# Transposing transfers begun by ScalarE's queue in place of SyncE's, in a fused windowed-attention and feed-forward kernel

## The chip, the cores and the metric

The kernel runs on one core of one Trainium2 chip. The metric is the device time of one execution in microseconds; lower is better. The profile shows the core's engines by these names: PE (TensorE matmuls) and PEld (its weight loads), DVE (VectorE), ACT (ScalarE), POOL (GpSimd) and SP (SyncE), which only begins transfers. `SPq` and `ACTq` are the instruction queues of SP and ACT.

## The reference

```python
scores = scale * q @ k.T                       # (8 batches, 8 heads, 576, 576), head size 64
rel = pos[:, None] - pos[None, :]
mask_plain = (rel >= 0) & (rel < 32)                          # heads 0 to 3
mask_dil = (rel >= 0) & (rel < 128) & (rel % 4 == 0)          # heads 4 to 7
attn = softmax(where(mask, scores, -1e9))
x = (attn @ v) as (8, 576, 512)
xn = (x - mean) / sqrt(var + 1e-6) * g
out = x + relu(xn @ w1) @ w2                   # w1 512 x 2048, w2 2048 x 512
```

Everything is float32 on the outside. Each query sees 32 keys: the 32 last ones, or every fourth of the last 128.

## The kernel before, in words

The 8 x 576 rows are 36 tiles of 128 rows, nine to a batch. A tile goes through the attention (scores, softmax, values), then through the layer norm (`norm`), and is then transposed, so that its 512 features stand on the partitions. Three tiles make a block, and the feed-forward part (`ffn`) works on blocks: `up` multiplies the transposed block with w1 into `ps_f` (L597), ACT evicts it with a relu as a 16-bit `hh` (L603) and DVE as the remainder `hl` (L604), and `down` multiplies with w2 (L620) and adds x (L626). `ps_f` has four PSUM buffers.

Products are made in 16-bit halves: a float32 number is a high part and a remainder. So `norm` ends with two tiles, `xh`, a cast by ACT (L568), and `xl`, the remainder, made by POOL (L569). `transposes` (L572 to L576) then moves both through two transposing DMA transfers into `xT`, which has two buffers by turns of blocks. The second one lies in spare room of the tile `w1_sb`, and is called `w_sb` in the profile. That makes 72 such transfers, two for each tile.

Around that run other users of the same queues. SP begins all loads and stores: queries and keys (L175 and L186, into `qk` or `slot`), values (L194), the weights (L655), small copies of v between tiles (L247), the results (L634), and the `row` loads (L225). These belong to `scale_v`: it takes the values of up to nine tiles, squares and sums them on ACT (L226), sums over the tiles on DVE (L228) and over the partitions on PE (L230), which gives a scale for the 16-bit values of the batch (`sv`). The `row` tile has two buffers and is also the tile that `down` writes its result to. ACT also splits weights and values (L153), casts queries and keys (L308, L279) and computes the exponentials (L413, L451, L452).

What order all this is in is settled in two steps. The kernel gives each piece of work (`unit`) a due time by hand and writes the pieces out in that order. A scheduler at build time then orders the instructions of each engine, by a simulation of the engines; each engine runs its own list strictly in order, DMA starts included, and waits at the head of the list until the semaphores of that instruction are there. Eight semaphores serve all transfers by turns, whichever engine begins them, so that a transfer also waits for the one eight before it.

Of the kernel before, what the change touches and what calls it, by code (L numbers as in the profile page):

```python
# [17 lines left out]
P = 128  # L18
# [50 lines left out]
def attention_then_ffn(ctx: ExitStack, tc, qkv, masks, g, w1, w2, out):  # L69
    nc = tc.nc  # L70
# [501 lines left out]
    def transposes(t, blk, i):  # L572
        st = state[t]
        blk["xTh"], blk["xTl"] = xT[blk["b"] % 2][:, 0], xT[blk["b"] % 2][:, 1]
        for name, src in (("xTh", st["xh"]), ("xTl", st["xl"])):
            nc.sync.dma_start_transpose(out=blk[name][:, :, i * P : (i + 1) * P], in_=src)  # L576


    def ffn(blk, apart):
# [186 lines left out]
    for b in range(NBLK):  # L766
        blk = dict(t0=b * NB, b=b)
        for i in range(NB):
            t = b * NB + i
            if t < EARLY:  # L770
                t_at = TIMES["E"][t]
                if t:
                    unit(f"L{t}", t_at - 8.0, lambda t=t: load_tile(t), f"V{t - 2}")
                else:
                    unit("L0", 0.5, load_first)
                for n, (name, what) in enumerate((
                    ("S", scores_early), ("M", softmax_early), ("V", values_early), ("N", norm),
                )):
                    unit(f"{name}{t}", t_at + 3.0 * n, lambda t=t, what=what: what(t), f"L{t}", f"{name}{t - 1}")
                unit(  # L780
                    f"T{t}", t_at + 10.0, lambda t=t, i=i, blk=blk: transposes(t, blk, i), f"N{t}",
                    f"P{NFC // NW2 - 1}" if b else None,
                )
                if t == EARLY - 1:
                    unit(f"A{t}", TIMES["X"], lambda t=t: split_last(t), f"v{t}", f"N{t}")
                continue
# [12 lines left out]
            if t % TPP == 5 and t + 4 < NT:  # L799
# [4 lines left out]
            do("N", VALUES + 2, norm, f"V{t}")  # L804
            unit(
                f"T{t}", t_at + READY, lambda t=t, i=i, blk=blk: transposes(t, blk, i),
                f"N{t}", f"P{NFC // NW2 - 1}" if b else None, f"b{b - 2}",
            )
# [24 lines left out]
        else:  # L833
            when = max(start, units[f"T{b * NB + NB - 1}"][0] + 0.1, max(units[a][0] for a in last))
            for n, (took, what) in enumerate(ups + downs):
                name = f"b{b}" if n == len(ups) + len(downs) - 1 else f"b{b}.{n}"
# [76 lines left out]
```

## Time and profile before

| | |
|---|---|
| runs | 941.67 us, median of 3 (940.76 to 941.94) |
| profiled execution | 944.02 us, its span 942.2 us |
| PE busy | 890.7 us, 95% |
| DVE, ACT, POOL busy | 634.2, 312.7, 312.3 us |
| DMA engines | 42.3% of 16 engines' span, all on one queue |
| transposing transfers | 72, all begun by SP |

Times inside the span count from its start. Engines work side by side, so busy times don't add up; a group's row names the line, the engine, what is written and read, how often, and in the bracket how long the engine stood idle before it and what ended that. Beginning a transfer is not counted as busy time of an engine. Clock stands for the granted TensorE clock, 1.00 at full speed.

### The profile page before, as it was taken

The page shows a single profiled execution, that of the slowest core. Times are in us where ns is not written, and L with a number is a line of the kernel's source. Part 1 is how long each engine was busy: PE and PEld are TensorE (multiplying, and loading weights), DVE is VectorE, ACT ScalarE, POOL GpSimd, SP SyncE. Part 2 cuts the span into 40 slices and gives each one's busy share as a digit, 9 for nine tenths or more (in the row PEclk, how much of TensorE's full clock was granted, in tenths as well). Part 3 has the DMA queues.
Part 4 walks back from the last instruction along what each step waited for, and adds up shares of the span by engine and source line. Part 5 has one row for each costly group of instructions (what it writes and reads, how often), then busy time and mean ns, then how long its engine had stood idle before and what let it go on. Part 6 is the DMA issues. An engine that isn't in the chain of part 4 may idle for free.

```text
span 942.2 us, 18610 instructions
## 1 busy us (share of the span) xinstructions
PE 890.7 (95%) x7608; PEld 552.2 (59%) x7608; DVE 634.2 (67%) x1379; ACT 312.7 (33%) x588; POOL 312.3 (33%) x319
## 2 busy tenths in 40 slices
PE   4479789999999999999999999999999999999998
PEld 4379466777665555565565565565565565564553
DVE  4799658896977577786686686686686685660210
ACT  4556742334323343251241451241241341130110
POOL 1010273646234235454253353354243341120000
PEclk9979899999999999999999999999999999999999
DMA  7887872754344516446143654364043411010000
GB/s 241 311 229 229 187 176 50 153 122 115 66 75 93 148 52 133 92 71 136 37 80 71 169 105 71 89 123 90 30 88 69 87 27 37 21 24 23 12 1 34
DMA packets 79622, 93.39 MB, mean 99 GB/s; under 512 B 47920, under 2 KB 53680, under 8 KB 79536
## 3 DMA queue, kind: packets, MB, share of 16 engines
q1 hardware_dynamic: 79536, 92.21, 42.3%
q8 instruction: 59, 0.97, 0.4%
q14 instruction: 27, 0.22, 0.1%
HBM read 71.86 MB, written 9.44 MB: 86 GB/s over the span
## 4 chain that ended last, share of the span: by engine, by line
PE 81%; DMA 10%; ACT 3%; DVE 3%; issue 2%; SPq 1%; POOL 1%; ACTq 0%; DVEq 0%; POOLq 0%
PE ps_f L597 36%; PE ps_f L620 35%; PE ps_s L330 4%; PE ps_v L528 4%; DMA row<-in_qkv 4%; DMA slot<-in_w 3%; DMA xT<-xl 1%; ACT row L226 1%; DMA slot<-in_qkv 1%; DMA v<-in_qkv 0%; PE ps_f L673 0%; ACT w_sb L153 0%; DVE slot L662 0%; POOL slot L280 0%; DVE slot L154 0%
## 5 line engine op out<-in xcount | busy, mean ns | idle before, releaser
L620 PE MATMUL ps_f<-w_sb,hh 128*128 128x512 f16 x1152 | 345.0, 380 | 5.8 <-ACT w_sb L153 5.0
L597 PEld LDWEIGHTS <-w_sb 128*128 128x128 f16 x3072 | 256.0, 99 | 126.6 <-issue 4.6
L620 PE MATMUL ps_f<-w_sb,hl 128*128 128x512 f16 x576 | 219.1, 380 | 0.0
L597 PE MATMUL ps_f<-xT,w_sb 128*128 128x384 f16 (+1 forms) x1536 | 199.2, 289 | 2.9 <-DMA xT<-xh 2.4
L597 PE MATMUL ps_f<-w_sb 128*128 128x384 f16 (+1 forms) x1536 | 196.7, 287 | 0.0
L620 PEld LDWEIGHTS <-hh 128*128 128x128 f16 x1152 | 111.8, 98 | 131.5 <-issue 6.8
L603 ACT ACTIVATE hh<-ps_f 128x384 f16<-128x384 f32 (+1 forms) x184 | 91.1, 500 | 216.8 <-PE ps_f L597 216.8
L604 DVE SCALAR_TENSOR_TENSOR hl<-ps_f,hh 128x384 f16<-128x384 f32 (+1 forms) x184 | 100.2, 569 | 42.4 <-ACT hh L603 40.3
L620 PEld LDWEIGHTS <-hl 128*128 128x128 f16 x576 | 56.5, 98 | 67.1 <-issue 1.8
L362 DVE TENSOR_TENSOR sc<-ps_s,mask 32x256 f32<-32x256 f32 x128 | 53.6, 419 | 51.2 <-PE ps_s L330 49.8
L435 DVE STREAM_TRANSPOSE pt_d<-pk 32x256 f32<-32x256 f32 x128 | 79.4, 621 | 1.8
L626 DVE SCALAR_TENSOR_TENSOR row<-ps_f,s,x 128x512 f32<-128x512 f32 x36 | 27.0, 749 | 74.5 <-PE ps_f L620 74.0
L446 POOL TENSOR_TENSOR sc<-sc,mx 128x512 f32<-128x512 f32 x32 | 33.4, 1043 | 116.3 <-DVE mx L444 116.3
L451 ACT ACTIVATE p<-sc 128x512 f32<-128x512 f32 x32 | 20.2, 631 | 128.2 <-POOL sc L446 128.2
L569 POOL TENSOR_TENSOR xl<-xn,xh 128x512 f16<-128x512 f32 x36 | 42.0, 1166 | 59.1 <-ACT xh L568 49.8
L330 PE MATMUL ps_s<-slot 128*128 128x128 f16 (+1 forms) x768 | 58.8, 226 | 2.1 <-DVE sc L348 2.1
L330 PEld LDWEIGHTS <-slot 128*128 128x128 f16 x768 | 50.9, 99 | 12.7 <-DVE sc L348 3.0
L287 POOL COPY slot<-slot 128x128 f16<-128x128 f16 x56 | 17.5, 340 | 119.4 <-PE ps_v L528 119.3
L348 DVE TENSOR_TENSOR sc<-ps_s,mask 32x256 f32<-32x256 f32 x128 | 53.5, 418 | 4.9 <-PE ps_s L330 3.4
L453 POOL TENSOR_TENSOR pk<-p,pk 128x512 f16<-128x512 f32 x32 | 40.7, 1271 | 45.8 <-ACT pk L452 45.8
L458 DVE STREAM_TRANSPOSE pt_b<-pk 32x128 f16<-32x128 f16 x87 | 26.1, 300 | 42.0 <-ACT pk L452 28.4
L554 POOL TENSOR_TENSOR rstd<-rstd,mhalf 128x1 f32<-128x1 f32 x36 | 21.1, 587 | 94.9 <-DVE rstd L553 85.2
(100 smaller groups left out, 961.3 us busy)
## 6 DMA issues: line engine op xcount, KB each, us to landing
qk<-in_qkv SPq DMA_DIRECT2D x36, 512.0 KB, 6.9
slot<-in_qkv SPq DMA_DIRECT2D x32, 512.0 KB, 6.7
slot<-in_w SPq DMA_DIRECT2D x14, 1024.0 KB, 6.3
out_x<-row SPq DMA_DIRECT2D x36, 256.0 KB, 2.0
row<-in_qkv SPq DMA_DIRECT2D x33, 256.0 KB, 2.9
v<-in_qkv SPq DMA_DIRECT2D x33, 256.0 KB, 3.0
slot<-in_w SPq DMA_DIRECT2D x4, 512.0 KB, 7.3
slot<-in_qkv SPq DMA_DIRECT2D x28, 64.0 KB, 4.5
```

The source lines that it names most:

```text
L330: nc.tensor.matmul(out, lhs, rhs, start=(n == 0), stop=(n == len(terms) - 1))
L348: nc.vector.tensor_tensor(out=sc[pj, 0:HP, :], in0=ps[pj, :, W * j : W * j + 2 * W], in1=mask_16[pj, m : m + 1, :].broadcast_to([W, HP, 2 ...
L362: nc.vector.tensor_tensor(out=sc[pj, HP:H, :].rearrange("p h (t i) -> p h t i", t=2), in0=ps[pj].rearrange("p h (t c) -> p h t c", t=2)[:, ...
L435: nc.vector.transpose(dd[pj].rearrange("p t h (i r) -> p r t h i", r=DIL)[:, j], pk[pj, HP:H, :].rearrange("p h (t i) -> p t h i", t=2),)
L446: nc.gpsimd.tensor_tensor(out=sm, in0=sc, in1=mx.broadcast_to([P, H, 2 * W]), op=ALU.subtract)
L453: nc.gpsimd.tensor_tensor(out=pk16[:, :, :, 1], in0=p32, in1=pk16[:, :, :, 0], op=ALU.subtract)
L528: nc.tensor.matmul(oo, l, r, start=(n == 0), stop=(n == len(mm) - 1))
L569: nc.gpsimd.tensor_tensor(out=xl, in0=xn, in1=xh, op=ALU.subtract)
L597: nc.tensor.matmul(z[:, n], l, r, start=(m == 0), stop=(m == len(mm) - 1))
L603: nc.scalar.activation(hh, z, AF.Relu)
L604: nc.vector.scalar_tensor_tensor(out=hl, in0=z, scalar=0.0, in1=hh, op0=ALU.max, op1=ALU.subtract)
L620: nc.tensor.matmul(o, l, r, start=(f == 0 and m == 0), stop=(f == NFC - 1 and m == 2))
```

## The change

The two transposing transfers of a tile are begun by ACT's queue; SP no longer begins any of them. What is moved, where to and when it is needed stay the same.

```diff
@@ def transposes(t, blk, i):
         st = state[t]
         blk["xTh"], blk["xTl"] = xT[blk["b"] % 2][:, 0], xT[blk["b"] % 2][:, 1]
         for name, src in (("xTh", st["xh"]), ("xTl", st["xl"])):
-            nc.sync.dma_start_transpose(out=blk[name][:, :, i * P : (i + 1) * P], in_=src)
+            nc.scalar.dma_start_transpose(out=blk[name][:, :, i * P : (i + 1) * P], in_=src)
```

The scheduler orders all engines anew, so lists change in more than the 72 rows. On ACT, behind the exponentials of the fourth tile (t=3, 111 us in the profile), where the third tile is transposed:

```order
-L603 ACTIVATE hh<-ps_f 128x4x128
-L153 ACTIVATE w_sb<-w_sb,s_2_1539 128x2x512
+L576 DMA_TRANSPOSE xT<-xh 128x4x128
+L603 ACTIVATE hh<-ps_f 128x4x128
+L576 DMA_TRANSPOSE xT<-xl 128x4x128
 L308 CAST slot<-qk_1329 128x1024
 L279 CAST slot<-qk_1329 128x4x128
 L279 CAST slot<-qk_1329 128x512
-L226 ACTIVATE row,v_sums<-row 128x512 x2
-L153 ACTIVATE w_sb<-w_sb,s_2_1539 128x2x512
+L153 ACTIVATE w_sb<-w_sb,s_2_1539 128x2x512 x2
+L226 ACTIVATE row,v_sums<-row 128x512 x2
```

The two transfers stand around an eviction, and the two squares L226 have moved behind both splits of w2. A little further on the same list, the same happens to the last three squares of the batch:

```order
 L423 COPY pt_a_81<-ps_s 128x256
 L425 COPY pt_d_85<-ps_s 128x64 x4
-L226 ACTIVATE row,v_sums<-row 128x512 x2
 L153 ACTIVATE w_sb<-w_sb,s_3_1541 128x2x512
-L226 ACTIVATE row,v_sums<-row 128x512
+L226 ACTIVATE row,v_sums<-row 128x512 x3
```

They now follow the last split. On SP, at the same place (108 to 113 us):

```order
 L225 DMA row<-in_qkv 128x512 x2
-L576 DMA_TRANSPOSE xT<-xh 128x4x128
-L186 DMA slot<-in_qkv 64x2x1024
-L576 DMA_TRANSPOSE xT<-xl 128x4x128
-L186 DMA slot<-in_qkv 64x2x1024
+L186 DMA slot<-in_qkv 64x2x1024 x2
 L247 DMA v_b_84<-slot 32x4x64
 L194 DMA v_1662<-in_qkv 128x512
```

The two halves of a load of queries and keys now follow the row loads directly. On SP at the start of the third batch's row loads (310 us):

```order
 L186 DMA slot<-in_qkv 64x2x1024 x2
-L576 DMA_TRANSPOSE xT<-xh 128x4x128
-L225 DMA row<-in_qkv 128x512
-L576 DMA_TRANSPOSE xT<-xl 128x4x128
-L225 DMA row<-in_qkv 128x512
+L225 DMA row<-in_qkv 128x512 x2
 L634 DMA out_x<-row 128x512
 L225 DMA row<-in_qkv 128x512 x7
```

The first two row loads no longer stand behind and between the transfers of that tile.

## The prediction

> **What bounds the kernel now.** I read the page's busy line and slices first, then TensorE stage by stage, then its waits and the chain that ended last, and last the queues and engines that the moved transfers leave and join.
>
> ```profile
> span 942.2 us, 18610 instructions
> PE 890.7 (95%) x7608; PEld 552.2 (59%) x7608; DVE 634.2 (67%) x1379; ACT 312.7 (33%) x588; POOL 312.3 (33%) x319
> ...
> 100.00:125.00 25.00, 20.39 (x134) 10.21 (x134) 10.88 (x11) 21.19 (x46) 11.81 (x9) 0.86 0.93 210
> 125.00:150.00 25.00, 20.39 (x273) 17.94 (x272) 19.66 (x50) 7.73 (x14) 10.86 (x12) 0.93 0.66 121
> ...
> 310.00:337.00 27.00, 24.41 (x160) 14.49 (x159) 14.67 (x34) 11.29 (x29) 3.88 (x5) 1.00 0.61 157
> 337.00:341.00 4.00, 4.00 (x17) 1.97 (x15) 1.97 (x8) 2.00 (x4) 1.41 (x2) 0.57 0.00 2
> 341.00:900.00 559.00, 559.00 (x4101) 322.69 (x4100) 376.32 (x832) 161.53 (x294) 192.91 (x188) 1.00 0.34 72
> ```
>
> The columns of a stage are its bounds, its length, the busy time of PE, PEld, DVE, ACT and POOL, the granted clock, the DMA share and GB/s. From 341 to 900 us TensorE is busy 559.00 of 559.00 us: nothing that happens on SP or in the DMA engines there can shorten the time, it can only add. What can be won behind the loading phase lies mainly in two small places: 4.6 us idle in 125 to 150 (25.00 less 20.39), and 2.6 us in 310 to 337, after which the clock is 0.57 for 4 us, another 1.7 us (4 x 0.43). Stage 100 to 125 stands out the other way: ACT, the engine that takes over the transfers, is busy 21.19 of 25.00 us, and the DMA engines 0.93.
>
> ```profile
> PE ps_f L620 <- ACT w_sb L153: 5.0, 1, 5.0
> PE ps_v L230 <- DVE x L486: 4.6, 1, 4.6
> ...
> PE ps_f L597 <- DMA xT<-xh: 2.4, 2, 1.8
> ...
> PE ps_v L230 <- DVE v_tot L228: 2.1, 1, 2.1
> ```
>
> TensorE's own waits say the same (us in total, times, longest): the moved transfers (xT) keep it waiting for 2.4 us in all, while the two matmuls L230, which add up the squares of v, cost 4.6 us at 128 us and 2.1 us at 335 us. Both L230 end a chain of `row` loads, and both chains pass through SP just where it begins a transposing transfer.
>
> **The moved instructions.**
>
> ```profile
> L576 SPq DMA_TRANSPOSE xT<-xh x18: 1199/1231/1563, 50.0 to 776.8; - x18
> L576 SPq DMA_TRANSPOSE xT<-xl x18: 1194/1244/2067, 51.6 to 778.1; - x18
> ...
> DMA to landing us min/median/max: 2.4/5.8/9.1
> ```
>
> With the two groups into the second buffer there are 4 x 18 = 72, each 1.2 us of SP's time (median), so 72 x 1.24 = 89 us leave SP and join ACT, whose 312.7 us become some 402, 43% of the span (the page leaves issues out of its busy time). ACT's own price for beginning one does not stand in this trace; the bounds are 0.33 us, the shortest plain issue on SP (the row loads below), and 2.07 us, the longest transposing one. I take 1.24, the same instruction's. What counts is not the sum but what is queued behind each: the eviction L603 that frees TensorE's `ps_f`, the squares L226, the splits L153.
>
> **From 341 us on: 0.** Place after place looks like this.
>
> ```profile
> 474.63 0.62 ACT L568 CAST xh<-xn 128x512 f16<-128x512 f32 x1 [2.06 <-DVE xn L563]
> 475.15 0.48 ACT L603 ACTIVATE hh<-ps_f 128x384 f16<-128x384 f32 x1
> 476.87 0.49 ACT L603 ACTIVATE hh<-ps_f 128x384 f16<-128x384 f32 x1 [1.24 <-PE ps_f L597]
> 478.10 0.63 ACT L451 ACTIVATE p<-sc 128x512 f32<-128x512 f32 x1 [0.74 <-POOL sc L446]
> ...
> 475.32 1.16 POOL L569 TENSOR_TENSOR xl<-xn,xh 128x512 f16<-128x512 f32 x1 [1.31 <-ACT xh L568]
> ...
> ACT hh L603 <- PE ps_f L597: 216.8, 119, 32.5
> ```
>
> xh is ready at 475.25 and xl at 476.48, so the two issues need ACT until 477.7 at the latest, with an eviction between them or 0.9 us late. ACT has waited for TensorE 216.8 us in front of its evictions, and with four `ps_f` buffers, one filled in 1.7 us (the evictions at 475.15 and 476.87), TensorE can run on for some 4 us: three fillings less the eviction itself and DVE's share in it. A late eviction of 1 to 2.5 us is therefore hidden; if POOL were late with xl by 5 us it would not be, and that would cost 1 to 3 us a time. I take 0, with +3 as the upper end.
>
> **50 to 104 us: 0.** The first two pairs leave SP in this stretch. The xT waits above (at most 2.4 us) could shrink, or ACT's splits behind the pairs come up to 2.5 us later (two issues). Both end at the 5.0 us for which TensorE waits for ACT's first split of w2 behind this stretch; that split hangs on weight loads which the release of a `slot` sets free, not SP's turn.
>
> **108 to 133 us: +0.9.** This is where the change is decided, on the third tile's pair.
>
> ```profile
> 108.36 1.24 SPq L576 DMA_TRANSPOSE xT<-xh  x1
> ...
> 110.36 1.22 SPq L576 DMA_TRANSPOSE xT<-xl  x1
> 111.64 0.61 SPq L186 DMA_DIRECT2D slot<-in_qkv  x1
> ...
> 115.41 0.94 SPq L225 DMA_DIRECT2D row<-in_qkv  x2
> 120.63 1.28 SPq L186 DMA_DIRECT2D qk<-in_qkv  x2
> 123.44 0.33 SPq L225 DMA_DIRECT2D row<-in_qkv  x1
> ...
> row<-in_qkv SPq DMA_DIRECT2D x33, 256.0 KB, 2.9
> ...
> L153 ACT ACTIVATE w_sb<-w_sb,s 128x1024 f16<-128x1024 f32 x8 | 9.0, 1145 | 0.0
> ...
> 114.67 0.63 ACT L226 ACTIVATE row<-row 128x512 f32<-128x512 f32 x1
> ...
> 119.99 1.05 ACT L308 CAST slot<-slot 128x1024 f16<-128x1024 f32 x1 [1.91 <-DMA slot<-in_qkv]
> ...
> 122.66 0.67 ACT L226 ACTIVATE row<-row 128x512 f32<-128x512 f32 x1
> ...
> 130.35 0.63 ACT L226 ACTIVATE row<-row 128x512 f32<-128x512 f32 x1 [5.28 <-DMA row<-in_qkv]
> ```
>
> SP's side gains: without 1.24 + 1.22 us the second half of `slot` begins at about 109.2 in place of 111.64. ACT's side loses. In front of the two L226 of 114.67 there now stand two issues (2.46) and one split L153 more (1.15), so they come at about 118.2. Their `row` buffers are what the two loads of 115.41 wait for, so these come at about 118.9. L308 then starts at 119.4 to 119.99, about as before, since its load is there earlier. In front of the next squares there now stand two splits more (2.3), so these start at 124.4 to 125.0 in place of 122.66, and the last row load, begun at 123.44, comes 1.8 to 2.3 us later. It was 6.9 us under way (123.44 to 130.35), against a median of 2.9, because two 512 KB `qk` loads begun at 120.63 went ahead of it. If all of that excess is queueing it lands when it did, or 0.3 us sooner, the transposes being out of its queue; if none is, it lands 2.3 us later. Most of it is (4.0 of 6.9), so I take +0.9 out of -0.3 to +2.3. TensorE stands at L230 until then and has little idle time afterwards, so the delay goes through to the end.
>
> **310 to 337 us: 0.**
>
> ```profile
> 309.48 1.34 SPq L186 DMA_DIRECT2D slot<-in_qkv  x2
> 311.93 1.23 SPq L576 DMA_TRANSPOSE xT<-xh  x1
> 313.21 0.66 SPq L225 DMA_DIRECT2D row<-in_qkv  x1
> ...
> 312.00:314.00 2.00, 2.00 (x12) 0.98 (x11) 1.24 (x5) 0.00 (x0) 1.90 (x2) 1.00 1.00 240
> ...
> 313.21 5.23 DMA row<-in_qkv
> ...
> 336.42 0.17 DVE v_tot L228
> ```
>
> Here SP holds the first of nine row loads behind a transposing transfer that waits for xh until 311.93. Without it the load begins at about 310.9 (309.48 and 1.34), 2.3 us earlier, and five loads one after the other in the same buffer carry that to L230. But the DMA engines are full (1.00) while it waits, with 1 MB of `slot` ahead of it, and it lands behind that in any case: the 2.3 us go into a longer landing than 5.23, and the transposing bytes are merely shared differently. Bounds: -3.8 (all of the 2.1 us wait and 1.7 us of clock) and +0.7 (xl's bytes, which stood behind the row, now go beside it). I take 0.
>
> **Sum.** 0 + 0.9 + 0 + 0 = +0.9 us on the profiled execution: 944.02 (942.2 of span and 1.8 around it) becomes 944.9. It lies 2.35 us above the median of the runs, 941.67, so the forecast in runs is 942.6 us.
>
> The Trainium skill, "DMA: Bandwidth & Descriptors", section "Issuing engines are not separate DMA queues", speaks against the change: transfers begun by different engines run on the same 16 DMA engines, and a second issuer saves issue time only. By it alone the loads gain SP's 2.46 us at the third pair and no bandwidth, which is what the full DMA engines at 312 us suggest; no run here has two issuers yet. Its section "Queues, rings and completion order" gives SP and ACT rings of their own, served in turn by packets; by that a transposing transfer would land nearer 2.4 than 5.8 us, which the sum has no use for beyond the 2.4 us of xT waits.
>
> **Rivals.**
>
> *SP is set free and the row chain starts earlier* (faster, 0.26). If the row at 313.21 is held by its place in the queue rather than by full DMA engines, TensorE's wait at L230 and the slow clock behind it go: -3.8 us, with the second place at its -0.3: 941.67 - 4.1 = 937.6. Half of it gives 939.6. For it: the chain that ended last goes through `SPq L576` at both places. Against it: the DMA share of 1.00.
>
> *ACT, working in order, becomes the bound of 100 to 133 us* (slower, 0.22). Its place is the two L226 behind the third pair; it decides as soon as the last row load keeps its 6.9 us from a later start. Price: +2.3 at L230, as much again as the low clock costs there now if the longer wait prolongs it (0.93 over 25 us, 1.7), +0.7 in the second row chain: 941.67 + 4.7 = 946.4.
>
> *A transposing transfer lands late on its new ring* (slower, 0.07).
>
> ```profile
> 234.13 5.85 DMA xT<-xl
> ...
> 240.03 0.81 PE ps_f L597 x4
> ```
>
> This one landed at 239.98, and TensorE took it up at 240.03. If taking turns with the loads' packets makes it 8 to 9 us, the longest landing above, instead of 5.85, TensorE loses 2 to 3 us: 942.6 + 2.5 = 945.1. Against it: it is the only landing of the 72 that stands in that chain behind the loading phase.
>
> *The change is mostly a new order of instructions* and the moved issues themselves weigh nothing: within the forecast.
>
> **How the numbers follow.** A measurement of this kernel tells about 0.2%, 1.9 us, from no change. The forecast, 941.5 to 943.5, has 0.45 and lies within that. Faster: the first rival, 0.26. Slower: 0.22 + 0.07 = 0.29. The range runs from 938.2, which takes in 85% of the first rival's 4.1 us, to the second rival's 946.4.
>
> **What would show it.** Right: 72 transposing issues of about 1.2 us in ACT's queue, TensorE still without idle time from 341 on, its wait at the L230 near 128 us about 1 us longer, the one near 335 about as long. Wrong: L226 before the last row load not later than 122.7, a first row at 313 that lands before 318, a clock of 1.00 behind L230, or evictions L603 for which TensorE waits.

## The result and the profile after

The changed kernel takes 958.0 us (median of 4 runs, 956.42 to 959.48) against 941.81 us before (940.76 to 943.78): the ratio is 1.0169, 95% interval 1.0144 to 1.0194. That is 16 us slower. The forecast was 942.6 us and the range ended at 946.4: the prediction was wrong, on the slower side.

The page of the kernel after: the span with the busy line, and the two DMA queues (packets, MB, share of 16 engines).

```profile
span 957.7 us, 18558 instructions
PE 895.5 (94%) x7608; PEld 553.7 (58%) x7608; DVE 636.1 (66%) x1379; ACT 311.9 (33%) x588; POOL 314.4 (33%) x319
...
q1 hardware_dynamic: 40368, 82.76, 33.1%
q10 hardware_dynamic: 39168, 9.45, 8.6%
```

The change did what it says: q10, ScalarE's own queue, is new and carries the 72 transposing transfers, 39168 / 72 = 544 packets each. TensorE executes the same 7608 matmuls. Its idle time grew from 942.2 - 890.7 = 51.5 to 957.7 - 895.5 = 62.2 us, by 10.7, and its busy time by 4.8: waits, and more time at half clock behind them.

Stages of the kernel after (length, busy PE, PEld, DVE, ACT, POOL; granted clock, DMA share, GB/s):

```profile
75.00:100.00 25.00, 22.41 (x443) 21.28 (x437) 21.95 (x44) 14.03 (x32) 2.00 (x2) 0.93 0.52 165
100.00:125.00 25.00, 19.17 (x132) 9.80 (x131) 13.11 (x12) 21.61 (x46) 13.03 (x9) 0.93 0.99 203
125.00:150.00 25.00, 19.91 (x225) 16.29 (x224) 16.18 (x45) 7.18 (x14) 11.93 (x12) 0.86 0.72 131
225.00:250.00 25.00, 18.95 (x202) 13.34 (x201) 15.85 (x34) 6.75 (x11) 13.28 (x12) 0.96 0.63 127
250.00:300.00 50.00, 50.00 (x393) 31.16 (x391) 37.14 (x85) 16.43 (x30) 18.34 (x18) 0.95 0.22 40
300.00:400.00 100.00, 94.12 (x692) 52.95 (x690) 67.88 (x155) 31.86 (x63) 37.47 (x39) 0.98 0.50 113
400.00:900.00 500.00, 499.61 (x3648) 288.00 (x3646) 337.93 (x750) 143.43 (x263) 169.85 (x165) 1.00 0.33 70
```

One stage stands out: 225 to 250 us, 6.05 us idle where the kernel before had 0.14,

```profile
225.00:250.00 25.00, 24.86 (x251) 17.08 (x249) 21.50 (x48) 9.09 (x16) 12.60 (x13) 1.00 0.47 96
```

and a clock of 0.96 and 0.95 in it and behind it. TensorE's waits in the kernel after from 225 to 600 us (total, times, longest):

```profile
PE ps_f L597 <- DMA xT<-xl: 6.1, 1, 6.1
PE ps_v L230 <- DVE v_tot L228: 2.9, 1, 2.9
...
PE ps_f L597 <- DVE hl L604: 1.2, 1, 1.2
```

How far it lags behind can be followed through the span: for each time of the kernel before, the time at which the other one has done the same share of the matmuls (columns summed up in the order of their ends), less that time, in us.

| at, in the kernel before | 75 | 100 | 150 | 225 | 250 | 300 | 350 | 400 | 900 |
|---|---|---|---|---|---|---|---|---|---|
| after | -1.3 | 0.6 | 3.3 | 3.6 | 12.0 | 11.6 | 13.9 | 14.5 | 15.4 |

8.4 of the 15.4 us are lost at one place, some 5 between 75 and 150 us (with a lead of 1.3 used up), and 3 between 300 and 400. What happens at the one place is in the timeline of the kernel after (start, duration):

```profile
235.06 1.15 POOL L569 TENSOR_TENSOR xl<-xn,xh 128x512 f16<-128x512 f32 x1
...
235.95 1.33 SPq L186 DMA_DIRECT2D qk<-in_qkv  x2
...
236.24 1.32 ACTq L576 DMA_TRANSPOSE xT<-xl  x1
...
243.17 0.33 PE L597 MATMUL ps_f<-xT,w_sb 128*128 128x384 f16 x1
...
249.55 1.44 PE L597 MATMUL ps_f<-xT,w_sb 128*128 128x384 f16 x4 [6.05 <-DMA xT<-xl]
```

ScalarE begins xl of tile 8 (tiles count from 0) 0.03 us after POOL has made it: nothing holds it up in ScalarE's list. It is the transfer that is slow. The DMA issues of the kernel before from 233 to 243 us, and of the kernel after from 235.2 to 250 us (KB each, median us to landing):

```profile
qk<-in_qkv SPq DMA_DIRECT2D x2, 512.0 KB, 6.5
...
xT<-xl SPq DMA_TRANSPOSE x1, 5.9
```

```profile
qk<-in_qkv SPq DMA_DIRECT2D x2, 512.0 KB, 11.0
...
xT<-xl ACTq DMA_TRANSPOSE x1, 13.3
```

Before, xl stood in SP's queue between the two 512 KB loads of q and k (they are tile 14's) and landed in 5.9 us. After, the two loads are on SP's ring (its own queue of packets, q1 above) and xl is on ScalarE's (q10), and all three are slow. Two-us windows of the kernel after:

```profile
240.00:242.00 2.00, 2.00 (x11) 0.91 (x10) 1.93 (x6) 0.00 (x0) 0.25 (x1) 1.00 1.46 153
242.00:244.00 2.00, 1.50 (x8) 0.59 (x6) 1.93 (x6) 0.00 (x0) 0.00 (x0) 1.00 0.66 94
244.00:246.00 2.00, 0.00 (x0) 0.00 (x0) 1.92 (x4) 0.00 (x0) 0.00 (x0) 1.00 0.24 51
...
248.00:250.00 2.00, 0.45 (x2) 0.25 (x2) 0.00 (x0) 0.00 (x0) 0.00 (x0) 0.56 0.08 22
```

From 244 to 246 us the packets move 51 GB/s, against 221 from 238 to 240, although neither xl nor the second load has landed. The 0.24 beside it is not the busy share: a window counts a packet where it starts, with its whole time, and so 1.46 can stand from 240 to 242 us. Counted by the time in which the packets ran, the engines are busy 0.50 from 244 to 246 us: half idle, and for the rest mostly held by packets that began earlier.

### The profile page after: what moved, and what is told of

The parts are those of the page before. It is cut to its first block, busy times and chain, and to the rows that moved or that the text cites. A ratio compares the mean times of both kernels' runs of the same rounds, so it can differ in the third digit from the quotient of the medians.

```text
span 957.7 us, 18558 instructions
## 1 busy us (share of the span) xinstructions
PE 895.5 (94%) x7608; PEld 553.7 (58%) x7608; DVE 636.1 (66%) x1379; ACT 311.9 (33%) x588; POOL 314.4 (33%) x319
## 3 DMA queue, kind: packets, MB, share of 16 engines
q10 hardware_dynamic: 39168, 9.45, 8.6%
## 5 line engine op out<-in xcount | busy, mean ns | idle before, releaser
L603 ACT ACTIVATE hh<-ps_f 128x384 f16<-128x384 f32 (+1 forms) x184 | 91.1, 500 | 235.6 <-PE ps_f L597 215.0
L604 DVE SCALAR_TENSOR_TENSOR hl<-ps_f,hh 128x384 f16<-128x384 f32 (+1 forms) x184 | 100.9, 569 | 58.2 <-ACT hh L603 56.2
```

The costliest lines, as they stand in the source:

```text
L603: nc.scalar.activation(hh, z, AF.Relu)
L604: nc.vector.scalar_tensor_tensor(out=hl, in0=z, scalar=0.0, in1=hh, op0=ALU.max, op1=ALU.subtract)
```

## The experiments

All of them compute the whole reference; only the queue of some transfers changes, and in one the size of packets. T stands below for the line that begins the transposing transfers. Ratios are against the kernel before (medians 942.1 to 943.1 us beside them).

### Which tiles make the loss

```diff
 e1, of the changed kernel
-            nc.scalar.dma_start_transpose(
+            (nc.sync if t == 8 else nc.scalar).dma_start_transpose(
 the others, of the kernel before
-            nc.sync.dma_start_transpose(
+            (nc.scalar if t == 8 else nc.sync).dma_start_transpose(        e2
+            (nc.scalar if t >= 9 else nc.sync).dma_start_transpose(        e3
+            (nc.sync if t >= 9 else nc.scalar).dma_start_transpose(        e4
+            (nc.scalar if t >= 13 else nc.sync).dma_start_transpose(       e7
+            (nc.scalar if 9 <= t <= 12 else nc.sync).dma_start_transpose(  e8
```

> As the changed kernel, but the two transposing transfers of tile 8 are begun by SP again; the other 70 stay with ScalarE. Theory R (one late landing): the changed kernel lost about 8.5 of its 16 us at one place, 225 to 250 us, where TensorE waits 6.05 us for the transfer xl of tile 8, which took 13.3 us to land on its own ring beside two 512 KB loads, and then runs 6.8 us at half clock. Then this kernel gives that back: about 949.5 us (958.0 - 8.5), TensorE idle at 225 to 250 us below 1 us. Rival O (loss spread over the program, from ScalarE's queue and from lists that the scheduler writes anew): one pair of 36 is worth next to nothing, 956 to 958 us.

> As the kernel before, but the two transposing transfers of tile 8 alone are begun by ScalarE. Theory R: the late landing comes with this one pair, 941.8 + 8.5 = about 950.3 us, with a TensorE wait of about 6 us for xl near 240 us. Rival O: the kernel before had slack there, 942 to 944 us.

> As the kernel before up to tile 8, with the transposing transfers of tiles 9 to 35 (27 of 36 pairs) begun by ScalarE. Theory R: identical to the kernel before until 250 us; behind it only what the changed kernel lost from 300 us on, about 2.5 us (2.0 at the row loads near 335 us, 0.4 near 575 us): 944.3 us, and 942 us if those 2 us near 335 came from where the work stood and not from the queue. Rival O: three quarters of the pairs carry three quarters of the loss, about 954 us.

> As the changed kernel up to tile 8 (9 of 36 pairs begun by ScalarE), with the transfers of tiles 9 to 35 on SP. Theory R: the loss up to 250 us is all there (3.8 us by 150 us, 8.5 us at 225 to 250 us): 941.8 + 12.3 = about 954 us. Rival O: a quarter of the loss, about 946 us.

> As the kernel before up to tile 12, transposing transfers of tiles 13 to 35 (23 of 36 pairs, from 354 us on) begun by ScalarE. Theory H (what tiles 9 to 35 cost came before 341 us: evictions that stand behind a transposing transfer in ScalarE's list, and the row loads): 942.9 us, up to 944 with the short waits seen near 376 and 560 us. Rival Q (each pair on ScalarE holds evictions, by the same amount all the way): 23/27 of the 7 us, about 949 us.

> As the kernel before, transposing transfers of tiles 9 to 12 alone (4 of 36 pairs, 256 to 316 us) begun by ScalarE. Theory H: nearly all of the loss of tiles 9 to 35, 946 to 950 us, with TensorE waits for DVE's hl near 264 and 333 us and for the scale of v near 339 us as in that kernel. Rival Q: 4/27 of 7 us, about 944 us.

| on ScalarE | us, median | ratio, interval |
|---|---|---|
| all but tile 8 (e1) | 950.29 | 1.0087 [1.0063, 1.0110] |
| tile 8 (e2) | 946.28 | 1.0035 [1.0009, 1.0061] |
| tiles 9 to 35 (e3) | 950.01 | 1.0088 [1.0071, 1.0105] |
| tiles 0 to 8 (e4) | 946.64 | 1.0051 [1.0031, 1.0071] |
| tiles 13 to 35 (e7) | 942.92 | 0.9993 [0.9969, 1.0016] |
| tiles 9 to 12 (e8) | 947.29 | 1.0052 [1.0035, 1.0068] |

Two of 72 transfers back on SP (e1) give back 7.7 of the 16 us, as theory R had it, and the stage is whole again:

```profile
225.00:250.00 25.00, 24.91 (x271) 17.72 (x269) 20.25 (x42) 7.65 (x13) 13.39 (x13) 1.00 0.57 119
```

The same pair alone (e2) costs less, 3.4 us: between the two theories. Its profiled run took 950.26 us, the second slowest of ten (943.40 to 952.86); TensorE waits 4.0 us there. So the transfer is probably not equally late in every execution, and a size is to be taken from the medians, not from the profile. R was wrong on the tiles behind: e3 loses 7 us, where it gave 2.5 at most, and e4 loses 4 us, where it gave 12 and rival O gave 4. e7 and e8 split the tiles of e3. The 46 transfers of tiles 13 to 35 cost nothing (theory H), with TensorE busy

```profile
350.00:600.00 250.00, 249.90 (x1840) 142.95 (x1837) 179.58 (x399) 78.94 (x145) 103.26 (x101) 1.00 0.48 99
600.00:900.00 300.00, 300.00 (x2154) 173.15 (x2152) 187.93 (x413) 77.45 (x140) 84.44 (x83) 1.00 0.24 50
```

in e7, and the eight of tiles 9 to 12 cost 4.9 us (0.0052 x 942.7). TensorE's waits of e8 from 250 to 400 us show where:

```profile
PE ps_v L230 <- DVE v_tot L228: 3.1, 1, 3.1
...
PE ps_f L597 <- DVE hl L604: 0.8, 1, 0.8
PE ps_v L528 <- DVE pt_a L434: 0.6, 2, 0.4
```

Evictions held in ScalarE's list (L604 follows L603) and what hangs on them (`pt_a` is a part of the exponentials, transposed by DVE) make 1.4 us: the two issues of tile 9, from 255.76 to 259.20, stand in front of a cast L308 that begins at 259.31, in the kernel before at 256.28. The wait for the row chain at L230 is 3.1 in place of 2.1. It is 2.9 to 3.1 in the six profiles with tile 12 on ScalarE and 2.1 to 2.7 in the other fourteen, so that 1 us goes with the change. Behind it this profile has 6.8 us at half clock in place of 3.4, another 1.7, and with it comes close to its lag of 4.0 us at 400 us. But that piece doesn't go with these tiles: e2, which leaves them on SP, has 6.8 us too, and e3, which moves them, 3.4.

e7 and e8 together don't reach e3 (0.9993 and 1.0052 against 1.0088, [1.0071, 1.0105]): 2 to 4 us of it are in neither and stay open.

### Why xl lands late

Each of these is the kernel before with a few queues exchanged around tile 8.

```diff
e5   tile 8's T, and the two qk loads of tile 14 (L186)      -> nc.scalar
e6   only the two qk loads of tile 14                        -> nc.scalar
e9   the same, and the v load of tile 13 (L194)              -> nc.scalar
e15  the same, and the three copies into v_b of tile 11 (L247) -> nc.scalar
e10  tile 8's T -> nc.scalar; the qk loads of tile 14 in four parts of 512 columns, 2 KB a row
e12  the changed kernel, and the two qk loads of tile 14     -> nc.scalar
```

> As the kernel before, but both the transposing transfers of tile 8 and the two 512 KB loads of q and k that go beside them (those of tile 14) are begun by ScalarE: one ring again, the other one, with both loads ahead of xl. Theory M (mixing): transposing packets of one ring and 4 KB load packets of the other crawl when an engine changes between them; on one ring they go one after the other, so xl lands in 6 to 9 us although both loads are ahead of it, and TensorE waits 0 to 3 us near 240 us: 942.9 to 945 us. Rival A (ScalarE's ring is slow for a transposing transfer, or loads ahead are what delays it): xl lands in 11 us or more, wait 4 us or more, 946 to 950 us.

> The mirror: as the kernel before, all transposing transfers on SP, but the two 512 KB loads of q and k beside tile 8's (those of tile 14) are begun by ScalarE. Theory M: two rings again, so xl on SP lands in 9 to 13 us, TensorE waits 3 to 6 us near 240 us, and the time is 946 to 951 us. Rival A (ScalarE's ring as such): xl is on SP's ring with no load ahead of it and lands in 3 to 6 us, no wait: 942 to 944 us.

> The mirror again, so that the packets do meet: as the kernel before, all transposing transfers on SP, but the v load of tile 13 and the two 512 KB q and k loads of tile 14, which stood around xl of tile 8, are begun by ScalarE, so that nothing but xl is in SP's ring. Theory M (mixing on two rings makes both crawl, whichever engine began which): xl lands in 9 to 13 us, TensorE waits 2 to 6 us near 240 us, 945 to 950 us. Rival A (a transposing transfer is slow only on ScalarE's ring): xl lands in 3 to 6 us, no wait, 942 to 944 us.

> The mirror with nothing but the two transposing transfers of tile 8 in SP's ring: beside the v load of tile 13 and the q and k loads of tile 14, the three copies into v_b of tile 11 are begun by ScalarE too. Theory M: packets of xl on SP's ring and 4 KB load packets on ScalarE's are in flight together, xl lands in 9 to 13 us, TensorE waits 2 to 5 us near 240 us, 945 to 949 us. Rival A (slow only where ScalarE began the transposing transfer and SP the loads): 3 to 7 us, no wait, 942 to 944 us.

> One size changed: as the kernel with only tile 8's transfers on ScalarE (946.3 us, xl landed in 11.3 us), but the q and k loads of tile 14 are cut into four of 256 KB whose packets are 2 KB instead of 4 KB; the bytes are the same. Theory M, in the form that each change of an engine from a load packet to a transposing one costs (from 233.5 to 241.5 us, 16 load packets on each engine: 0.5 us for a pair): 32 pairs of 0.4 us, xl lands in 14 to 16 us, TensorE waits 7 to 9 us, about 950 us. Rival B (the engines' time is shared by bytes): xl lands in 10 to 12 us as before, about 946 us.

> As the changed kernel (958.0 us), all 72 transposing transfers on ScalarE, but the two 512 KB loads beside tile 8's xl are begun by ScalarE too. Theory M: xl of tile 8 lands in 6 to 8 us and the wait of 6.05 us near 243 us is gone, as if tile 8 had gone back to SP: about 950 us. Rival A (ScalarE's ring as such): 956 to 958 us.

| xl on | the two loads on | xl landed, us | us, median | ratio, interval |
|---|---|---|---|---|
| SP (before) | SP | 5.9 | 942.7 | |
| ScalarE (e2) | SP | 11.3 | 946.28 | 1.0035 [1.0009, 1.0061] |
| ScalarE (e5) | ScalarE | 6.7 | 942.38 | 0.9994 [0.9967, 1.0021] |
| SP (e6) | ScalarE | 7.1 | 943.16 | 1.0006 [0.9987, 1.0024] |
| SP (e9) | ScalarE | 7.3 | 943.28 | 1.0012 [0.9993, 1.0030] |
| SP (e15) | ScalarE | 12.4 | 944.39 | 1.0024 [0.9996, 1.0053] |
| ScalarE (e10) | SP, 2 KB rows | 7.1 | 944.19 | 1.0011 [0.9996, 1.0026] |
| ScalarE, all tiles (e12) | ScalarE | 7.9 | 951.45 | 1.0095 [1.0063, 1.0127] |

The landings are those of the one profiled execution of each kernel, the times medians of its runs. The issues of e2 and of e5:

```profile
qk<-in_qkv SPq DMA_DIRECT2D x2, 512.0 KB, 9.6
...
xT<-xl ACTq DMA_TRANSPOSE x1, 11.3
```

```profile
qk<-in_qkv ACTq DMA_DIRECT2D x2, 512.0 KB, 6.1
...
xT<-xl ACTq DMA_TRANSPOSE x1, 6.7
```

With both loads ahead of it on ScalarE's ring, xl is in the worst place of a queue, and still lands 4.6 us sooner than on a ring of its own; the loads gain 3.5 us too. So neither ScalarE's ring nor the loads ahead are the cause. e12 does the same inside the changed kernel and gives back 6.5 us; the wait of 6.05 us is down to 0.9.

The mirror has three forms. In e6 and e9 xl on SP's ring stood behind a v load or small copies, which were shared out against the big loads; the transposing packets only moved once these were through, so next to nothing was mixed, and both theories missed the landing (7.1 and 7.3 us); the times are those that rival A gave. With the ring cleared (e15) they did meet. The issues of e15, and TensorE's wait there:

```profile
qk<-in_qkv ACTq DMA_DIRECT2D x2, 512.0 KB, 10.2
...
xT<-xl SPq DMA_TRANSPOSE x1, 12.4
```

```profile
PE ps_f L597 <- DMA xT<-xl: 5.2, 1, 5.2
```

The crawl comes with SP's ring for the transposing transfer just as with ScalarE's, as theory M said of the landing and the wait; rival A falls. Its time is another matter: the profiled run, 950.86 us, is the slowest of ten (940.22 to 950.86), and the interval of the ratio reaches 0.9996, so a cost in the median isn't shown for e15.

e10 met neither expectation. With rows of 2 KB instead of 4 xl landed in 7.1 us, not in 14 to 16 and not in 10 to 12:

```profile
qk<-in_qkv SPq DMA_DIRECT2D x4, 256.0 KB, 7.0
...
xT<-xl ACTq DMA_TRANSPOSE x1, 7.1
```

So the form of theory M in which each change from one ring to the other has a fixed price doesn't hold. The size of the load's packets seems to decide, but that rests on one profile: the four loads also take SP 2.9 us to begin, where the two took 1.3, and the times of e10 and e2 have overlapping intervals.

The record of the single packets tells more. From the first load's issue to the landing of xl the longest 4 KB packet of the loads lasted 3.3 us in the kernel after, 3.4 in e2 and 3.5 in e15, against 1.8 in the kernel before, 1.1 in e6, 0.9 in e5 and e9, and 0.5 in e12; in e10 the longest 2 KB packet lasted 1.1 us. The median one took 0.3 us or less in all of them. So part of the crawl is that some packets of the loads last for microseconds while packets of the other ring run. Why they do stays open; the traces don't show the single engines.

### The start, the rows and the evictions, one by one

```diff
e11  T of tiles 0 to 7  -> nc.scalar   (the rest of this block likewise, in the kernel before)
e16  T of tile 2
e13  T of tile 12
e14  T of tiles 9 and 10
```

> As the changed kernel up to tile 7 (8 of 36 pairs begun by ScalarE), SP again from tile 8 on: step 3 of the prediction alone, without tile 8. The prediction's step: +0.9 us, 943.6 us. Rival E (the start carries the 3.2 us that the changed kernel's profile shows by 150 us): 946 us. Rival F (what the start shows is chance: profiles of one and the same start differ by up to 5 us at 150 us): 942 to 943.5 us.

> As the kernel before, but the two transposing transfers of tile 2 alone (108 and 110 us) are begun by ScalarE: step 3 of the prediction by itself, the squares behind the splits and the last row load later. Step 3: +0.9 us, 943.8 us, last square 0.5 to 1.9 us later. Rival (the whole of the start's loss sits here): +3 to +5 us, 946 to 948 us. Rival F (chance): 942 to 943 us, last square no later against the end of TensorE's work before it.

> As the kernel before, but the two transposing transfers of tile 12 alone (312 and 314 us, between SP's first row loads) are begun by ScalarE: step 4 by itself. Step 4 of the prediction: 0, bounds -3.8 to +0.7, so 942.9 us. Rival (a) of the prediction (SP set free brings the row chain forward): the wait of 2.05 us near 336 us goes, 939 to 941 us. Theory K (the row chain runs from buffer to buffer, not from SP's queue, and the evictions held by the transfers push it back): wait 2.5 to 3 us, 944 to 945 us.

> As the kernel before, but the transposing transfers of tiles 9 and 10 alone (256 to 266 us) are begun by ScalarE: the evictions by themselves. Theory H: the wait for DVE's hl near 264 us and for pt_a near 282 us come back, 0.8 + 0.4 us, and what they cost further on: 944 to 945.5 us. Rival (the 0.5% of tiles 9 to 12 is made at the row loads): 942.9 us.

| on ScalarE | us, median | ratio, interval |
|---|---|---|
| tiles 0 to 7 (e11) | 948.60 | 1.0064 [1.0046, 1.0083] |
| tile 2 (e16) | 944.85 | 1.0023 [1.0004, 1.0042] |
| tile 12 (e13) | 947.02 | 1.0042 [1.0020, 1.0064] |
| tiles 9 and 10 (e14) | 943.13 | 1.0010 [0.9991, 1.0029] |

Tile 2 alone (e16) costs 2.2 us, more than the step's +0.9 and less than the rival's 3 to 5. Its transfers land as late as that of tile 8. Its issues from 110 to 127 us, beside the loads of q, k, v and rows, and TensorE's wait from 100 to 150 us:

```profile
xT<-xh ACTq DMA_TRANSPOSE x1, 13.4
xT<-xl ACTq DMA_TRANSPOSE x1, 13.3
```

```profile
PE ps_f L597 <- DMA xT<-xh: 3.5, 1, 3.5
```

On SP the two took 6.0 and 7.0 us (kernel before). The wait of 4.6 us at L230, which the prediction had there, is gone in this profile: TensorE comes so late that the rows are in time. So one wait stands in place of another, and the lag of this profile behind the kernel before is 2.7 us at 100 us and 2.5 at 150. The late landing is shown; that it makes the 2.2 us of the medians is not.

e11 loses 6 us, all of rival E and more, and can't be split further by profiles: what the kernel before has done at 163.8 us is done at 160.6 to 169.5 us in the five profiles with these tiles on ScalarE, and at 159.2 to 163.8 in the twelve with them on SP. Nor do the costs add up here: e4 moves all the tiles of e11 and tile 8 besides, and costs no more (1.0051 against 1.0064).

e14 shows the evictions: a wait of 0.5 us for DVE's hl and of 0.4 for pt_a, in runs +0.9 us, not told from zero. e13 misled. Tile 12 alone seemed to cost 4 us, nearly as much as tiles 9 to 12 together, but in its profile beginning xh took ScalarE 6.75 us, with an eviction behind it; these are e13's rows:

```profile
312.96 6.75 ACTq L576 DMA_TRANSPOSE xT<-xh  x1
...
321.07 0.49 ACT L603 ACTIVATE hh<-ps_f 128x384 f16<-128x384 f32 x1 [8.14 <-PE ps_f L597]
```

It wasn't a wait for a semaphore: xh was ready at 312.93, and the waits for semaphores in front of the two transfers lasted 0.04 us at most. What held the issue isn't shown; the first packet of xh moved at 319.68, when the loads of q and k begun on SP at 310.52 had landed (318.73). In the changed kernel the same transfer was begun in 1.22 us. What tile 12 costs there isn't settled by e13; e8 less e14 leaves some 4 us for tiles 11 and 12.

### The places put together

```diff
e17  (nc.sync if t in (2, 8, 12) else nc.scalar).dma_start_transpose(...)
e18  (nc.sync if t in (1, 2, 8, 9, 10, 11, 12) else nc.scalar).dma_start_transpose(...)
```

> As the changed kernel (958.0 us), with three of 36 pairs of transposing transfers back on SP: those of tiles 2, 8 and 12; 33 pairs stay with ScalarE. Theory S (the loss sits where a transposing transfer meets big loads just before its data are needed): 958.0 - 7.7 (tile 8) - 2.2 (tile 2) - 3 (tile 12) = about 945 us, of which 1 us is the evictions behind tiles 9 to 11. Rival O (the loss is spread, tile 8 was the only place): 948 to 950 us.

> As the changed kernel, with seven of 36 pairs back on SP: tiles 1, 2 and 8 to 12; tiles 0, 3 to 7 and 13 to 35, 29 pairs, stay with ScalarE. Theory S: as the kernel before, 942.5 to 943.5 us, since what is left on ScalarE is covered. Rival (the rest of the start costs too): 945 us or more. A gain by SP set free would show as 941 us or less.

| on SP | us, median | ratio, interval |
|---|---|---|
| tiles 2, 8, 12 (e17) | 945.54 | 1.0028 [1.0012, 1.0045] |
| tiles 1, 2, 8 to 12 (e18) | 943.17 | 1.0011 [0.9994, 1.0027] |

The forecasts of theory S came true in both. Three of 36 pairs carry 0.0169 - 0.0028 = 1.4% of the 1.7% lost, and with seven back on SP no difference from the kernel before is shown. No kernel was found that is faster than the one before.

## Why the prediction was wrong, point by point

**The stretch without a term: 133 to 310 us.** The sum has steps for 50 to 104, 108 to 133, 310 to 337 and from 341 on. Between them it put nothing, and so took it that a transposing transfer lands as it did; the only reason near it, "the transposing bytes are merely shared differently", was given for 310 to 337 us. This is the step that failed: xl of tile 8 landed in 13.3 us instead of 5.9, at the only landing behind the loading phase for which TensorE had no slack. The row that told it, 239.98 against 240.03, stood in the prediction as a rival with a chance of 0.07 and a price of 2.5 us. Its place was right, and so were the loads beside it as the cause; that single packets of the loads would last 3 us was in no row. Its chance was too small, since nothing in a trace with one ring could exclude it, and its price was bounded by "the longest landing above", 8 to 9 us: a landing of the old arrangement is no bound for the new one. Measured: 7.7 us (958.0 less e1), a wait of 6.05 us and the 6.8 us at half clock that follow it.

**The order around it.** Taking xl out of SP's list also let the scheduler begin both loads before it, where it stood between them. That didn't matter by itself: e5 has both loads ahead on one ring, and no wait.

**From 341 us on, 0: right.** e7 gives 0.9993 [0.9969, 1.0016] with 46 of 72 transfers moved. TensorE is busy 549.90 of the 550 us from 350 to 900 us there.

**108 to 133 us, +0.9: mis-sized, and where the loss sits is open.** The rows did move as worked out, the first ones less than priced, the last one more. These are the squares of the kernel after:

```profile
116.33 0.61 ACT L226 ACTIVATE row<-row 128x512 f32<-128x512 f32 x1
...
123.92 0.65 ACT L226 ACTIVATE row<-row 128x512 f32<-128x512 f32 x1
...
132.20 0.63 ACT L226 ACTIVATE row<-row 128x512 f32<-128x512 f32 x1 [6.92 <-DMA row<-in_qkv]
```

They were forecast at 118.2 and 124.4 to 125.0; the last came 1.85 us later than before (130.35), inside -0.3 to +2.3. The two issues hardly delayed ScalarE's work here: they ran beside activations (the first, at 107.80, beside a split begun at 107.68). In e16 what TensorE waits for first is tile 2's transfer, 13.4 us under way; in the kernel after it landed as late (13.7 us), and TensorE, itself later, waits for the rows. Tile 2 alone costs 2.2 us, and the lag of the kernel after grows from 0.6 us at 100 to 3.3 at 150.

**50 to 104 us, 0: not settled.** Tiles 0 and 1 were not run alone; e11 loses 6 us over tiles 0 to 7, of which e16 explains 2.2, and e17 and e18, which differ by tiles 1 and 9 to 11, by 1.6 us with overlapping intervals.

**310 to 337 us, 0: the reason was right, the sum was short.** SP set free brings nothing, as said: the first square of this stretch came at 319.85 us in e8, which lags 1.5 us by then, against 318.46 before. Rival (a), "SP is set free", is refuted there, and no run shows its gain. But the term belonged to tiles 9 to 12 as a whole, which cost 4.9 us: 1.4 of evictions and what hangs on them, 1.0 more at L230, and a rest that no run explains, since the longer half clock of that profile shows without these tiles too. The evictions were priced only from 341 us on, where they are covered; ahead of it, where TensorE is just as full, they are not quite.

**Rival (b), ScalarE in order as the bound of 100 to 133 us:** not shown. Its sign is there in part: the last row load began at 124.69 in place of 123.44 and took 7.5 us to the square in place of 6.9. But the wait at L230 did not grow by its price of 2.3 us (4.0 in place of 4.6).

**What would show it.** The 72 issues are there,

```profile
L576 ACTq DMA_TRANSPOSE xT<-xh x18: 1205/1207/2433, 49.3 to 792.2; - x18
...
DMA to landing us min/median/max: 2.4/6.0/13.7
```

at the price taken, 1.2 us. The wait at the first L230 was to become 1 us longer and was 4.0 us in place of 4.6; the second was to stay and grew from 2.1 to 2.9. Of the signs named as wrong only the last came, and small: TensorE waits 1.2 us for an eviction (hl, which follows L603). They did not include the one that mattered, a longer landing: the median of all 72 is 6.0 us against 5.8, and only the longest, 13.7 against 9.1, tells it.

The page "DMA: Bandwidth & Descriptors" of the Trainium skill has, in its section "Queues, rings and completion order", that each DMA engine takes turns between the rings at packet granularity. By it I expected an earlier landing on a ring of its own. That did not come: the shortest landing is 2.4 us on either ring, and beside the big loads it was 13.3 us. Whether the engines take turns as the page says, these traces don't show; packets of both rings do start within the same microsecond. Its section "Issuing engines are not separate DMA queues" spoke against the change, and no gain in bandwidth was seen (98 GB/s over the span, 99 before).

## What to carry to other kernels

Moving a transfer to another engine's queue changes its ring, and with it what its packets run beside: before moving one, look at which big transfers are under way when it lands, and at the slack of its reader, not only at the time that the issuing engine gains or loses. A duration from the trace holds for the arrangement it was measured in; a landing time on one shared ring bounds nothing on two. If a small transfer that is soon needed must share the engines with big loads, leave it on their ring ahead of a part of them; cutting the loads' packets smaller helped too, in the one profile that tried it.

## What the runs showed of the hardware

- A transposing transfer on one ring and 512 KB loads with 4 KB rows on the other slow each other down: 11.3 to 13.3 us for the former and 9.6 to 11.0 (medians of two) for the loads, against 5.9 and 6.5 on one ring, while single 4 KB packets of the loads lasted up to 3.5 us (0.3 us is their usual time). It is so whichever engine began which (12.4 us in the mirror). With 2 KB rows it was 7.1 us, in one profile.
- It is probably not as long in every execution: ten runs of the mirror lie between 940.2 and 950.9 us, and the longest was the one profiled. The landings of the others aren't on record.
- The half clock comes in pieces of 3.4 us behind a wait of TensorE, but the wait's length doesn't settle how many: one piece behind 4.0 us (e2), two behind 6.05 (after), and behind the L230 near 335 us one (2.1 us, before; 2.9, after), two (3.1, e8; 2.7, e2) or none (3.1, e13; 3.0, e1).
- An issue of a transposing transfer takes 1.2 us of ScalarE's queue (median; 2.4 at most in the kernel after) and runs beside an activation already begun; what stands behind it waits, 3 us for the two issues of tile 9 in e8. In e13 one lasted 6.75 us, with its semaphores met.
